# The first attention batch in PSUM slots of three half score tiles with two squares on GpSimd, in place of the fused add-and-relu in h by seven products

## Chip, cores and metric

The kernel runs on one core of a Trainium2 chip. The metric is device time in microseconds (us). Most executions of a kernel agree within 0.3%.

## What is computed

Inputs are q, k and v of shape (8, 12, 448, 64), all fp32, and two weights: moe_w_in (768 x 2048) and moe_w_out (2048 x 768).

```python
scores = (1.0 / np.sqrt(64)) * np.matmul(q, k.transpose(0, 1, 3, 2))
attn = np.maximum(scores, 0.0) ** 2 / 448
x = np.matmul(attn, v)                      # per batch and head
x = x.transpose(0, 2, 1, 3).reshape(8 * 448, 12 * 64)
h = x @ w_in
r = np.maximum(h, 0.0)
out = (r * r) @ w_out                       # (3584, 768) fp32
```

## The kernel before

The kernel works in fp16 with fp32 accumulation. The twelve heads of a batch are three units of four heads, so there are 24 units; a unit has 7 row groups (J = 7). One score tile `t` is one row group of one unit: 128 partitions x two halves (`hh`) x 448 columns. For each, TensorE computes the scores in a PSUM slot (L255), ScalarE evicts them with relu into an fp16 tile `at` (L259), VectorE squares that tile in place (L372), and TensorE multiplies it with v ("AV round", L273 for batch 0, L320 for the others). The AV result is scaled into `xt`, the transposed x of the batch. A score is built of 64 x 64 matmuls, four of which use different quarters of TensorE.

**Batch 0.** q and k of units 0 to 5 are loaded in fp16 by GpSimd's DMA queue (`load16`, L91 to L96; the DMA converts from fp32) and turned by TensorE transposes (`pe_transpose`, L207), which are copied out of PSUM by VectorE (L217). The loop at L792 makes eleven visits of two score tiles. Each `visit` (L374) issues the scores of its tiles twice (`score(t, 2)`, L390), turns units 1 and 2 in between, then runs up to three AV rounds of tiles at least two visits old (`av_some`, L290), and squares the new tiles. Score slots have two PSUM banks, and there are three of them: two of the pool `sps`, one of `third`. The two AV accumulators have one bank each. Between visits 0, 2 and 5 the loop issues the next loads on GpSimd: q and k of units 3, 4 and 5, v of units 3, 4 and 5, and the four parts of w_in (`load_w1`, two DMAs each, L133).

**From batch 0 to the steady part.** After the loop, unit 3 is turned (L807), and weights and later units are loaded. The last AV rounds are interleaved with the first products of h (L827 to L836); then `visit([NB0, NB0 + 1])` issues the first scores of batch 1.

**h and the output.** h of batches 0 and 1 is a plain product (`h_group`, L415). From batch 2 on, h uses seven products instead of eight (`h_period`, L472) over sums of the blocks of w_in and x. There are two periods per batch and so 12 in all, each with 14 steps of six matmuls (L552). A step ends by evicting or adding an accumulator. `plus` (L492) adds a PSUM accumulator and a kept fp32 tile into `g`; it uses a special VectorE operation (L495) that clamps the sum between 0 and 3.4e38, so that relu is part of the addition. `rest` (L499) queues the square of two finished rows of g (L501). Then `o_groups` (L610) multiplies g with w_out (L739), also by seven products, for pairs of batches.

**What sets the order.** The whole program order is written out by hand (`manual_schedule`, L59): each engine, and each DMA queue, runs its instructions in the order in which the code issues them. From L841 on, a planner merges TensorE's steps with events at given times. VectorE's squares are kept in two queues with due times and costs: `due` for the attention squares and `due_g` for those of g. `fill` (L358) puts them where the planned VectorE time has room, `due` first; `flush` and `flush_g` put what must be done.

Of the kernel before, what the change touches and what calls it, by code (L numbers as in the profile page):

```python
# [10 lines left out]

FP16 = mybir.dt.float16
# [6 lines left out]
def kernel(  # L19
# [47 lines left out]
    g_p = ctx.enter_context(tc.tile_pool(name="gp", bufs=1))  # L67
    early = ExitStack()
    q16_p = early.enter_context(tc.tile_pool(name="q16p", bufs=3))

    PSUM = bass.MemoryType.PSUM
    s_p = ctx.enter_context(tc.tile_pool(name="sps", bufs=2, space=PSUM))
    first = ExitStack()
    third_p = first.enter_context(tc.tile_pool(name="third", bufs=1, space=PSUM))
    rounds = ExitStack()
    av_ps = [rounds.enter_context(
        tc.tile_pool(name=f"av{i}ps", bufs=1, space=PSUM, side="right"))
# [3 lines left out]
    def heads(t, n):  # L81
        b, u = divmod(n, NU)
        return t[b].rearrange(
            "(hh u hp) (p j) d -> u (hp p) hh (j d)", hh=2, hp=2, j=J)[u]
# [3 lines left out]
    blks: dict = {}  # L88
    qkt: dict = {}

    def load16(n):  # L91
        tq = q16_p.tile([P, 2, J * D], FP16, name="q16", tag="q16")
        tk = q16_p.tile([P, 2, J * D], FP16, name="k16", tag="k16")
        nc.gpsimd.dma_start(out=tq, in_=heads(q, n))
        nc.gpsimd.dma_start(out=tk, in_=heads(k, n))
        q16s[n] = (tq, tk)  # L96

    def load_v(n):
        t = v_p.tile([P, 2, J * D], FP16, name="vt", tag="vt")
# [51 lines left out]
        dst, x, y = ((t1, b12, b11), (t3, b22, b12), (t2, b22, t1), (nt4, b21, t2))[op]  # L151
        nc.vector.tensor_sub(dst[:, c], x[:, c], y[:, c])

    load16(0)
    ident = const_p.tile([P, P], FP16, name="ident", tag="ident")
    make_identity(nc, ident)
    zeros = const_p.tile([P, S], FP16, name="zeros", tag="zeros")
    nc.vector.memset(zeros, 0.0)
    junk = const_p.tile([P, 1], FP16, name="junk", tag="junk")
    nc.scalar.activation(out=junk, in_=zeros[:, 0:1], func=AF.Relu)  # L160
    load16(1)
    load_v(0)
    load16(2)
    load_v(1)
    load_v(2)

# [23 lines left out]

    big: list = []
    wsum: dict = {}
    slot_no = [0]

    def slot(dtype):
        slot_no[0] += 1
        third = not big and slot_no[0] % 3 == 2 and slot_no[0] < 29
        return (third_p if third else s_p).tile(
            [P, 2, 2048 // mybir.dt.size(dtype)], dtype, name="slot", tag="slot")

    def warm(n):
        ps = slot(FP32)
        for _ in range(n):
            nc.tensor.matmul(ps[:, 0, 0:S], lhsT=zeros[:, 0:P], rhs=zeros,  # L204
                             start=True, stop=True)

    def pe_transpose(n):  # L207
        srcs = q16s.pop(n)
        ts = new_qkt()
        ps = None if n > 3 else slot(FP16)  # L210

        def copy(i, act=False):
            dst, ps = ts[i].rearrange("p j c -> p (j c)"), pss[i][:, i if n < 4 else 0, 0:J * P]
            if act:
                nc.scalar.activation(out=dst, in_=ps, func=AF.Copy)
            else:
                nc.vector.tensor_copy(dst, ps)  # L217

        if n > 3:
            pss = [mm_tile(None, FP16).rearrange("p (i c) -> p i c", i=1) for _ in range(2)]  # L220
        else:
            pss = [ps, slot(FP16) if n == 0 else ps]
        for i, src in enumerate(srcs):
            for j in range(J):
                for hh in range(2):
                    nc.tensor.transpose(  # L226
                        pss[i][64 * hh:64 * hh + 64, i if n < 4 else 0, j * P:(j + 1) * P],
                        src[:, hh, j * D:(j + 1) * D], ident)
            if n == 0:
                copy(i)  # L230
                warm(1)
        qkt[n] = ts
        if n == 3:
            return lambda: (copy(0, True), copy(1))
        if n > 0:
            copy(0, n > 3)
            copy(1)


    xts: dict = {}  # L240
    ats: dict = {}
    seen: dict = {}
    now = [0]
    av_order: deque = deque(range(NU * J))
    avt = [None]

    def score(t, times=1):
        n, j = divmod(t, J)
        qT, kT = qkt[n]
        ps = slot(FP32)  # L250
        for hh in list(range(2)) * times:
            r = slice(64 * hh, 64 * hh + 64)
            for hp in range(2):
                c = slice(64 * hp, 64 * hp + 64)
                nc.tensor.matmul(  # L255
                    ps[c, hh, 0:S], lhsT=kT[r, j, c], rhs=qT[r, :, c],
                    start=True, stop=True)
        at = at_p.tile([P, 2, S], FP16, name="at", tag="at")
        nc.scalar.activation(out=at, in_=ps[:, :, 0:S], func=AF.Relu, scale=SK)  # L259
        ats[t] = at  # L260
        seen[t] = now[0]

    def av_round(t):
        n, j = divmod(t, J)
        b, u = divmod(n, NU)
        vt, at = vts[n], ats.pop(t)
        if j == 0:
            avt[0] = [p.tile([P, 512], FP32, name="avt", tag="av") for p in av_ps]
        ap = avt[0]
        for hp in range(2):  # L270
            r = slice(64 * hp, 64 * hp + 64)
            for hh in range(2):
                nc.tensor.matmul(  # L273
                    ap[hp][64 * hh:64 * hh + 64, 0:S],
                    lhsT=vt[r, hh, j * D:(j + 1) * D], rhs=at[r, hh, :],
                    start=(j == 0), stop=(j == J - 1))
        if j == J - 1:
            if u == 0:
                xts[b] = x_p.tile([P, NM, S], FP16, name="xt", tag="xt")
            for hp in range(2):  # L280
                dst = xts[b][:, 2 * u + hp, :]
                if b < 2 and u == NU - 1 and hp == 0:
                    nc.scalar.activation(
                        out=dst, in_=ap[hp][:, 0:S], func=AF.Copy, scale=CX)
                else:
                    nc.vector.tensor_scalar(  # L286
                        out=dst, in0=ap[hp][:, 0:S],
                        scalar1=CX, scalar2=None, op0=ALU.mult)

    def av_some(lag=2, most=3):  # L290
        done = 0
        while av_order and done < most:
            t = av_order[0]
            if t not in seen or seen[t] > now[0] - lag:
                break
            av_order.popleft()
            av_round(t)
            done += 1
            if t % J == J - 1:
                break  # L300

    unit = [NU]

# [66 lines left out]
    def square(at, lag=0.0):  # L370
        due.append((at_pe[0] + lag, 0.54,
                    lambda: nc.vector.tensor_mul(at, at, at), 0))  # L372

    def visit(tiles, turn=None, lag=2, most=3):  # L374
        now[0] += 1
        for t in tiles:
            if t % J == 0 and t >= NPE * J:
                prefetch(t // J + 2)
        if big:
            for t in tiles[:1]:  # L380
                score(t)
            av_unit()
            for t in tiles[1:]:
                score(t)
            at_pe[0] += 0.19 + 0.19 * len(tiles)
            for i, t in enumerate(tiles):
                square(ats[t], 0.6 + 0.85 * i)
            return
        for t in tiles:
            score(t, 2)  # L390
        if turn is not None:
            pe_transpose(turn)
        flush()
        av_some(lag, most)
        for t in tiles:
            square(ats[t])
        flush()


    gts: dict = {}  # L400
# [71 lines left out]
    def h_period(b, i0, extra):  # L472
# [17 lines left out]
            keep[s, nm] = t.rearrange("p (r c) -> p r c", r=2)  # L490

        def plus(s, y, nm, hi, right):  # L492

            now_ve(0.54)
            nc.vector._custom_dve(  # L495
                TENSOR_ADD_SAT, out=gs(s, hi, right), in0=acc(s, y),
                in1=keep[s, nm], s0=3.4e38, s1=0.0)

        def rest(g, lag):  # L499
            due_g.append((at_pe[0] + lag, 0.54,  # L500
                          lambda: nc.vector.tensor_mul(g, g, g), b))  # L501

        def relu21(s):
            nc.scalar.activation(out=gs(s, True, False), in_=acc(s, 0), func=AF.Relu)  # L504
            rest(gs(s, True), 0.8)

        def c12(s):
            plus(s, 1, "u2", False, True)
            rest(gs(s, False), 0.0)

        def left(k, f, m):

# [274 lines left out]


    NB0 = NU * J
    warm(10)  # L790
    pe_transpose(0)
    for i in range(11):  # L792
        visit([t for t in (2 * i, 2 * i + 1) if t < NB0], turn={1: 1, 4: 2}.get(i))
        if i == 0:
            load16(3)
            load_w1(0)
            load_w1(1)
            load_v(3)
        if i == 2:
            load16(4)  # L800
            load_w1(2)
            load_v(4)
        if i == 5:
            load16(5)
            load_w1(3)
            load_v(5)
    later = pe_transpose(3)  # L807
    load_v(6)
    load_w2(b11, 0, 0)
    load_w2(b12, 0, 1)  # L810
# [4 lines left out]
    first.close()  # L815
    big.append(ctx.enter_context(tc.tile_pool(
        name="mma", bufs=2, space=PSUM, reuse_waits="tile")))

# [2 lines left out]
    def some(part):  # L823
        for _, fn, _ in part:
            fn()

    av_some(1, 9)  # L827
    some(f0[0:2])
    later()
    av_some(0, 9)  # L830
    rounds.close()
    big.append(ctx.enter_context(tc.tile_pool(
        name="mmb", bufs=2, space=PSUM, side="right", reuse_waits="tile")))
    some(f0[2:4])
    some(f1[0:2])
    visit([NB0, NB0 + 1])  # L836

    T_G = NM * 0.1892
# [123 lines left out]
```

## Time and profile before

| | us |
|---|---|
| median of 3 runs (372.5 to 372.99) | 372.75 |
| the profiled execution's own time | 372.5 |
| its span in the profile | 370.7 |
| busy: TensorE matmul | 361.1 |
| busy: VectorE | 266.0 |
| busy: ScalarE | 247.7 |
| busy: GpSimd | 107.1 |
| L259 score evictions, 168 | 145.9, 0.919 each |
| L372 attention squares, 168 | 99.3, 0.618 each |
| L495 additions with relu, 72 | 0.62 each |
| L501 squares of g, 48 | 28.8, 0.618 each |
| L286 xt copies of batch 0, 5 on VectorE | 0.615 each |

Times in the views are microseconds from the start of the span. A line of a timeline gives start, length, engine, line of the kernel, operation, output and inputs with shapes, and the count of instructions merged into it; the bracket at its end is the idle time before it and what ended that. A line of a table by stretches gives the stretch, its length, the engine's busy time in it with the count of instructions, TensorE's granted clock as a share of the full one, the load of the DMA engines and GB/s. PE is TensorE's matmul, PEld its weight load, DVE is VectorE, ACT is ScalarE, POOL is GpSimd.

### The profile page before, as it was taken

Reading aid. Unit: us, or ns where it says so; the run is one execution under the profiler, and the core shown is the slowest. Engines: PE = TensorE matmul, PEld = TensorE weight load, DVE = VectorE, ACT = ScalarE, POOL = GpSimd, SP = SyncE. Lnnn points to the kernel's source line nnn. Section 1 sums busy time; section 2 is a strip of 40 time slices with the busy share of each in tenths; the row PEclk is TensorE's granted clock in tenths of the full one; section 3 lists DMA queues with packets and bytes.
Section 4 is the critical chain, followed back from the end, with each engine's and each line's share of the span. In section 5 each row is a group of like instructions: output and inputs, shape, how many; then the busy total and the mean of one; then the engine's idle time right before and its main releaser. Section 6 shows DMA issues by size and latency. Waiting matters only on the chain.

```text
span 370.7 us, 8742 instructions
## 1 busy us (share of the span) xinstructions
PE 361.1 (97%) x3600; PEld 230.9 (62%) x3600; DVE 266.0 (72%) x470; ACT 247.7 (67%) x370; POOL 107.1 (29%) x128
## 2 busy tenths in 40 slices
PE   8999999999999999999999999999999999999994
PEld 3554444445555778875555588887555689986663
DVE  1886677996767878798575766989756686884442
ACT  2997895786667999876555588887665885532220
POOL 8545531747542355522054045050000000000001
PEclk9999999999999999999999999999999999999998
DMA  8999999999999999969799999592233300002333
GB/s 116 195 204 205 205 204 170 126 146 161 190 170 137 185 106 104 108 90 73 137 136 108 176 162 94 82 104 48 54 82 88 87 1 2 2 0 79 91 91 83
DMA packets 121158, 42.63 MB, mean 115 GB/s; under 512 B 100832, under 2 KB 117760, under 8 KB 121120
## 3 DMA queue, kind: packets, MB, share of 16 engines
q0 software_dynamic: 82912, 23.01, 63.7%
q1 hardware_dynamic: 38048, 18.98, 25.8%
q8 instruction: 28, 0.46, 0.5%
q10 hardware_dynamic: 160, 0.10, 0.1%
q14 instruction: 10, 0.08, 0.1%
HBM read 45.61 MB, written 11.01 MB: 153 GB/s over the span
## 4 chain that ended last, share of the span: by engine, by line
PE 90%; ACT 4%; DVE 3%; issue 1%; POOL 0%; POOLq 0%; ACTq 0%
PE mm L739 34%; PE mm L552 27%; PE slot L255 10%; PE mm L423 9%; PE slot L320 7%; ACT at L259 4%; DVE at L372 1%; PE slot L204 1%; PE slot L226 1%; DVE xt L286 1%; PE mm L226 0%; DVE kT L217 0%; ACT u L641 0%; DVE osb L646 0%; PE avt L273 0%
## 5 line engine op out<-in xcount | busy, mean ns | idle before, releaser
L259 ACT ACTIVATE at<-slot 128x896 f16<-128x896 f32 x168 | 145.9, 919 | 27.9 <-PE slot L255 27.8
L372 DVE TENSOR_TENSOR at<-at 128x896 f16<-128x896 f16 x168 | 99.3, 618 | 12.1 <-ACT at L259 12.0
L109 POOL DMA_DIRECT2D qs<-in_q_dram x36 | 35.3, 983 | 116.5 <-DMA qT<-qs 108.7
L739 PEld LDWEIGHTS <-s 128*128 128x128 f16 x440 | 41.5, 98 | 32.7 <-issue 3.6
L255 PE MATMUL slot<-qT,kT 64*64 64x448 f16 x756 | 57.4, 360 | 1.6 <-ACT at L259 0.9
L552 PEld LDWEIGHTS <-w 128*128 128x128 f16 x576 | 54.3, 98 | 5.1 <-issue 4.3
L552 PE MATMUL mm<-xt,w 128*128 128x224 f16 x432 | 48.9, 259 | 0.0
L739 PEld LDWEIGHTS <-g 128*128 128x128 f16 x336 | 31.7, 98 | 24.1 <-issue 4.7
L552 PEld LDWEIGHTS <-ws 128*128 128x128 f16 x432 | 40.3, 98 | 4.7 <-issue 4.7
L646 DVE SCALAR_TENSOR_TENSOR osb<-mm,u 128x384 f32<-128x384 f32 (+1 forms) x30 | 16.2, 543 | 36.2 <-ACT u L641 23.7
L739 PE MATMUL mm<-b,g 128*128 128x384 f16 x224 | 40.7, 326 | 0.0
L739 PE MATMUL mm<-b,s 128*128 128x384 f16 x216 | 39.6, 326 | 0.2 <-DVE s L608 0.2
L423 PE MATMUL mm<-xt,w 128*128 128x448 f16 x192 | 39.8, 354 | 0.0
L739 PE MATMUL mm<-t,s 128*128 128x384 f16 x224 | 39.3, 326 | 0.0
L255 PEld LDWEIGHTS <-kT 64*64 64x64 f16 x756 | 19.6, 104 | 28.9 <-issue 23.6
L109 POOL DMA_DIRECT2D ks<-in_k_dram x36 | 35.1, 977 | 8.4 <-DMA b<-in_moe_w_out_dram 5.8
L575 POOL DMA_DIRECT2D out_dram<-osb x2 | 1.1, 564 | 119.7 <-DVE osb L646 119.7
L641 ACT ACTIVATE u<-mm 128x384 f32<-128x384 f32 x28 | 13.8, 492 | 31.3 <-PE mm L739 26.8
L552 PE MATMUL mm<-x,ws 128*128 128x224 f16 x288 | 34.1, 259 | 0.0
L495 DVE CUSTOM_DVE_ANT_0 g<-mm,m 128x448 f16<-128x448 f32 x36 | 22.4, 622 | 14.9 <-PE mm L552 7.2
L320 PE MATMUL slot<-at,vt 64*64 64x448 f16 x588 | 31.9, 350 | 0.2 <-DVE at L372 0.2
L501 DVE TENSOR_TENSOR g<-g 128x896 f16<-128x896 f16 x48 | 28.8, 618 | 0.4 <-ACT g L504 0.4
(68 smaller groups left out, 378.1 us busy)
## 6 DMA issues: line engine op xcount, KB each, us to landing
out_dram<-osb SPq DMA_DIRECT2D x52, 192.0 KB, 3.0
vt<-in_v_dram POOLq DMA_DIRECT2D x24, 224.0 KB, 6.0
qs<-in_q_dram POOLq DMA_DIRECT2D x36, 112.0 KB, 4.4
ks<-in_k_dram POOLq DMA_DIRECT2D x36, 112.0 KB, 5.2
w<-in_moe_w_in_dram POOLq DMA_DIRECT2D x8, 384.0 KB, 11.7
b<-in_moe_w_out_dram POOLq DMA_DIRECT2D x4, 768.0 KB, 17.1
q<-in_q_dram POOLq DMA_DIRECT2D x6, 224.0 KB, 7.6
k<-in_k_dram POOLq DMA_DIRECT2D x6, 224.0 KB, 8.1
```

The lines of the kernel that those rows point to most:

```text
L109: nc.gpsimd.dma_start(out=t[:, :, hh, :], in_=heads(src, n)[:, hh].rearrange("p (j d) -> p j d", d=D))
L255: nc.tensor.matmul(ps[c, hh, 0:S], lhsT=kT[r, j, c], rhs=qT[r, :, c], start=True, stop=True)
L259: nc.scalar.activation(out=at, in_=ps[:, :, 0:S], func=AF.Relu, scale=SK)
L320: nc.tensor.matmul(ps[64 * hh:64 * hh + 64, hp, 0:S], lhsT=vt[r, hh, j * D:(j + 1) * D], rhs=at[r, hh, :], start=(j == 0), stop=(j == J - 1))
L372: lambda: nc.vector.tensor_mul(at, at, at), 0))
L423: nc.tensor.matmul(cell[0][:, 0:S], lhsT=w1[f // 4][:, m, (f % 4) * P:(f % 4 + 1) * P], rhs=xts[b][:, m, :], start=(m == 0), stop=(m == NM ...
L495: nc.vector._custom_dve(TENSOR_ADD_SAT, out=gs(s, hi, right), in0=acc(s, y), in1=keep[s, nm], s0=3.4e38, s1=0.0)
L501: lambda: nc.vector.tensor_mul(g, g, g), b))
L552: nc.tensor.matmul(XY[s][y][:, r * Q:(r + 1) * Q], lhsT=left(k, i0 + 2 * s + r, m), rhs=right(k, m), start=(fresh and r == 0 and m == 0), ...
L641: nc.scalar.activation(out=t, in_=X[0][:, 0:HALF], func=AF.Copy, scale=CO)
L646: nc.vector.scalar_tensor_tensor(out=osb[row][:, c], in0=acc[0][:, 0:cc.stop - cc.start], scalar=CO, in1=keep[nm][:, cc], op0=ALU.mult, op ...
L739: nc.tensor.matmul(acc[0][:, 0:HALF], lhsT=left()[:, f], rhs=right[:, f], start=(fresh and f == 0), stop=(f == KH - 1), skip_group_check=n ...
```

## The change

There are two parts. **In h by seven products**, `plus` becomes an ordinary tensor addition, and `rest` queues a relu in SBUF (`tensor_scalar` with max) ahead of each square. After `relu21` it covers only the half that ScalarE has not already put through relu (448 elements per partition), after `c12` both halves (896).

**Batch 0** gets an order of its own in place of the loop of visits. The scores of a unit are 14 halves, packed into slots of three halves (three PSUM banks; two such slots), with one slot of two halves per unit: 15 slots in all. Each slot is evicted by one ScalarE instruction and squared by one instruction, on GpSimd for slots 1 and 3. Unit 0 begins with the seven first halves, so q and k of unit 0 are loaded in two DMAs each, and its first halves are turned and copied apart from its second halves. The transposes of units 0 to 2 use the banks of the AV accumulators. Slots 0 to 4 and slot 14 issue their scores once, the others twice. The AV rounds, `xt` copies and squares stand at written-out places; the first xt half of units 1 and 2 is copied by ScalarE. The pool `sps` is opened only after the first batch's slots are given back. Of the first h products, four instead of two stand ahead of unit 3's transposes, and the last two AV rounds of unit 2 come behind h's first six matmuls.

```diff
     def plus(s, y, nm, hi, right):
-
             now_ve(0.54)
-            nc.vector._custom_dve(
-                TENSOR_ADD_SAT, out=gs(s, hi, right), in0=acc(s, y),
-                in1=keep[s, nm], s0=3.4e38, s1=0.0)
-
-        def rest(g, lag):
-            due_g.append((at_pe[0] + lag, 0.54,
-                          lambda: nc.vector.tensor_mul(g, g, g), b))
+            nc.vector.tensor_add(gs(s, hi, right), acc(s, y), keep[s, nm])
+
+        def rest(g, relu, lag):
+
+            t = at_pe[0] + lag
+            due_g.append((t, 0.32 if relu is g else 0.2, lambda: nc.vector.tensor_scalar(
+                out=relu, in0=relu, scalar1=0.0, scalar2=None, op0=ALU.max), b))
+            due_g.append((t, 0.54, lambda: nc.vector.tensor_mul(g, g, g), b))
...
+    for n, sizes in enumerate(((2, 3, 3, 3, 3), (3, 3, 3, 3, 2), (3, 3, 3, 3, 2))):
+        order = ([(n, j, hh) for hh in range(2) for j in range(J)] if n == 0 else
+                 [(n, j, hh) for j in range(J) for hh in range(2)])
...
+    def new_slot():
+        return s3_p.tile([P, 3, 512], FP32, name="s3", tag="s3")
...
+    def score0(i, ps=None, times=1):
+        ps = new_slot() if ps is None else ps
+        w = len(halves[i])
+        at = at0_p.tile([P, w, S], FP16, name="at0", tag=f"at0_{i}")
+        for _ in range(times):
+            for o, (n, j, hh) in enumerate(halves[i]):
+                qT, kT = qkt[n]
+                r = slice(64 * hh, 64 * hh + 64)
+                for hp in range(2):
+                    c = slice(64 * hp, 64 * hp + 64)
+                    nc.tensor.matmul(
+                        ps[c, o, 0:S], lhsT=kT[r, j, c], rhs=qT[r, :, c],
+                        start=True, stop=True)
+        nc.scalar.activation(out=at, in_=ps[:, 0:w, 0:S], func=AF.Relu, scale=SK)
...
+    def square0(*slots):
+        for i in slots:
+            eng = nc.gpsimd if i in ON_POOL else nc.vector
+            eng.tensor_mul(at0[i], at0[i], at0[i])
...
+    def av0(n, j0, j1):
...
+        for j in range(j0, j1):
             for hp in range(2):
...
+                    nc.tensor.matmul(
+                        ap[hp][64 * hh:64 * hh + 64, 0:S],
+                        lhsT=vt[r, hh, j * D:(j + 1) * D],
+                        rhs=at_of[n, j, hh][r, :],
+                        start=(j == 0), stop=(j == J - 1))
...
-    warm(10)
-    pe_transpose(0)
-    for i in range(11):
-        visit([t for t in (2 * i, 2 * i + 1) if t < NB0], turn={1: 1, 4: 2}.get(i))
...
+    ON_POOL = (1, 3)
...
+    warm(ps, 10)
+    turn(0, (0,))
+    turn_copy(0, 0, LO_P)
+    turn_copy(0, 1, LO_P, slice(0, 2), act=True)
+    turn_copy(0, 1, LO_P, slice(2, J))
+    warm(ps, 2)
+    score0(0, ps)
+    score0(1)
+    turn(0, (1,))
+    turn_copy(0, 0, HI_P)
+    turn_copy(0, 1, HI_P)
+    square0(0)
+    score0(2)
+    square0(1)
+    start_all(load16(3))
+    load_w1(0)
+    load_w1(1)
+    load_v(3)
+    score0(3)
+    square0(2)
+    score0(4)
+    turn(1)
...
+    start_all(load16(4))
+    load_w1(2)
+    load_v(4)
+    square0(3)
+    score0(5, times=2)
...
+    score0(8, times=2)
+    av0(0, 0, 4)
+    square0(8)
+    score0(9, times=2)
+    av0(0, 4, 7)
+    x0(0, 0)
+    x0(0, 1)
+    square0(9)
+    score0(10, times=2)
+    av0(1, 0, 3)
...
+    score0(14)
+    square0(13, 14)
     load_v(6)
...
-    av_some(1, 9)
-    some(f0[0:2])
+    av0(2, 0, 3)
+    some(f0[0:4])
+    av0(2, 3, 5)
+    later = pe_transpose(3)
+    some(f1[0:2])
+    av0(2, 5, 7)
+    x0(2, 0, act=True)
+    x0(2, 1)
     later()
-    av_some(0, 9)
...
-    some(f0[2:4])
-    some(f1[0:2])
     visit([NB0, NB0 + 1])
```

## The prediction

> **What bounds the kernel now.** I read the page first, then the start of each engine's timeline, then VectorE by stage.
>
> The page: TensorE is busy for 97% of the span and carries 90% of the chain that ended last; VectorE and ScalarE are at 72% and 67%.
>
> ```profile
> span 370.7 us, 8742 instructions
> PE 361.1 (97%) x3600; PEld 230.9 (62%) x3600; DVE 266.0 (72%) x470; ACT 247.7 (67%) x370; POOL 107.1 (29%) x128
> PE 90%; ACT 4%; DVE 3%; issue 1%; POOL 0%; POOLq 0%; ACTq 0%
> ```
>
> So from the first h products on, a microsecond moves the end only if it makes TensorE wait or work. The first batch is the other case. ScalarE's timeline shows one unbroken row of 21 score evictions from 8.26 to 26.26 us:
>
> ```profile
> 8.26 8.27 ACT L259 ACTIVATE at<-slot 128x896 f16<-128x896 f32 x10 [6.02 <-PE slot L255]
> 16.87 3.35 ACT L259 ACTIVATE at<-slot 128x896 f16<-128x896 f32 x4 [0.34 <-PE slot L255]
> 20.48 5.78 ACT L259 ACTIVATE at<-slot 128x896 f16<-128x896 f32 x7 [0.27 <-PE slot L255]
> ```
>
> That is 0.827 us each with 0.6 us of gaps: ScalarE bounds the first 26 us. TensorE then reaches the first scores of the second batch (from there on it is full) at 28.57:
>
> ```profile
> 27.70 0.93 PE L423 MATMUL mm<-xt,w 128*128 128x448 f16 x4
> 28.57 0.57 PE L255 MATMUL slot<-qT,kT 64*64 64x448 f16 x8
> ```
>
> The third view is GpSimd's timeline, since the change puts arithmetic into that queue:
>
> ```profile
> 9.79 0.70 POOL L135 DMA_DIRECT2D w<-in_moe_w_in_dram  x1
> 11.22 0.67 POOL L135 DMA_DIRECT2D w<-in_moe_w_in_dram  x1 [0.73 <-DMA vt<-in_v_dram]
> 12.46 0.66 POOL L135 DMA_DIRECT2D w<-in_moe_w_in_dram  x1 [0.57 <-DMA q<-in_q_dram]
> 13.58 0.66 POOL L135 DMA_DIRECT2D w<-in_moe_w_in_dram  x1 [0.46 <-DMA k<-in_k_dram]
> ...
> 20.28 0.66 POOL L135 DMA_DIRECT2D w<-in_moe_w_in_dram  x1 [1.05 <-DMA w<-in_moe_w_in_dram]
> 22.52 0.71 POOL L100 DMA_DIRECT2D vt<-in_v_dram  x1 [1.58 <-DMA w<-in_moe_w_in_dram]
> ```
>
> Number the loads in program order. The 13th (second half of the first w) waits for the 5th (v of unit 0), the 14th for the 6th (q), the 15th for the 7th (k), the 20th for the 12th (w), the 21st (v of unit 4, at 22.52) for the 13th (w). Each load is issued only once the load eight before it has landed, and GpSimd stands still meanwhile. The transfers run at 200 to 206 GB/s from 15 us to 50 us, so these waits are paced by bytes, not by anything the change shortens.
>
> Last, VectorE by stretch (its busy time in each): h of batches 2 and 3, the start and the rest of the products after it, the same for 4 and 5, h of 6 and 7:
>
> ```profile
> 120.00:164.00 44.00, 35.75 (x66) 1.00 1.10 119
> 164.00:176.00 12.00, 10.24 (x20) 1.00 0.85 78
> 176.00:208.00 32.00, 20.96 (x38) 1.00 1.03 136
> 208.00:252.00 44.00, 33.55 (x63) 1.00 0.98 119
> 252.00:264.00 12.00, 11.43 (x21) 1.00 0.05 10
> 264.00:293.00 29.00, 18.55 (x34) 1.00 0.31 75
> 293.00:329.00 36.00, 27.80 (x51) 1.00 0.08 21
> ```
>
> It is 76 to 81% busy in h and up to 95% (11.43 of 12 us) just behind it, with 11 us to spare later in each output stage. In none of these h stages does TensorE wait for VectorE.
>
> **What the Trainium skill says.** *GPSIMD Engine Reference*, Performance versus the Vector engine: a two-input tensor operation on GpSimd takes about 2.6 cycles per element, 4497 ns for 2048 fp32. The trace of before has no such operation; an estimate for 1344 elements is 4497 x 1344/2048 = 2.95 us. *VectorE: DVE Perf Modes*, the perf-mode tier table: a single-source operation on 16-bit SBUF data runs at four elements a cycle, 693 ns for 2048; the trace agrees (the undisturbed copy of 128x2048 at L593 took 684 ns). *TensorE: Matmul & The Clock Gate*, Part 1: a TensorE that idles past some 3.4 us falls to half rate for about as long again. The trace agrees on the two rates: the ten warm-ups take 3.92 us (0.39 each), the same 448 columns later 1.24 us for six (0.21).
>
> **The change, part by part.**
>
> *Start of the first batch.* The four half loads let kT follow after seven transposes instead of fourteen. TensorE is busy warming up till 5.08 us in both kernels. Then I take 0.5 us for the transposes of q, 0.4 for k, 0.6 for the last copy (L217: 0.62), 0.5 for scores and waits: the first eviction at about 6.8 instead of 8.26, 1.4 us earlier. The third slot needs the second halves (transposes behind slot 1's scores, then two copies of 0.62), which costs about 0.9 us back.
>
> *Evictions.* 21 of 128x896 become 12 of 128x1344 and 3 of 128x896. One of 448 columns takes 0.544 (L283), one of 896 takes 0.919 (L259), so 448 columns more cost 0.375, and a wide one in a row 0.827 + 0.375 = 1.20 us. 12 x 1.20 + 3 x 0.827 = 16.9 against 21 x 0.827 = 17.4: 0.5 us saved, and one xt copy more on ScalarE (0.54) takes it back. The scores issued once instead of twice, and the two warm-ups, lie under ScalarE: nothing, as long as ScalarE is the bound.
>
> *The two squares on GpSimd.* Each takes 0.62 us off VectorE, which was not the bound: nothing gained. But GpSimd's queue is in program order. Slot 1's square stands behind the eleven first loads (two issues more than before at 0.7 us each: about 9.7 us) and ahead of q of unit 3. It lasts to 12.7; the transfers queued by then last to about 16 us, so they hardly run dry. **Slot 3's square stands behind v of unit 4.** That is now load 23 and waits for load 15, which is the same second half of the first w: the same bytes are ahead of it, so it is again issued at about 22.5. The square then runs from 22.5 + 0.7 = 23.2 to about 26.1. Bounds: 1.2 us of work (one element a cycle at the page's 1.2 GHz) to 4 us, so an end between 24.4 and 27.2; I take the two-input price.
>
> *Who waits for it.* The AV rounds 0 to 3 of unit 0 stand on TensorE between the scores of slots 8 and 9, and need the second halves of rows 1 to 3: slot 3. TensorE comes there at about 17 us and stops until 26.1. Behind it stand the scores of slots 9 to 14, so ScalarE runs dry too, at about 18.
>
> *Restart, at half rate for three microseconds or so.* Eleven matmuls of the AV rounds in three groups of four at 0.37: 27.2. Slot 9's scores, two groups: 28.0; its eviction ends at 29.0. AV rounds 4 to 6 and slot 10's scores: 30.1; evictions of slots 10 to 13 from 30.3, four at 1.20: 35.1; the xt copy 0.54; slot 14 (two halves) 0.83: **36.4 against 26.26**.
>
> *Handover.* Before, the transposes of unit 3 ran beside the last evictions. Now the first h products come first, in a PSUM bank of slot 14 that its eviction must free, and the transposes, two h products and the last AV rounds queue behind. After the last eviction TensorE has 6 h products (1.2), 4 AV rounds (0.8) and 28 transposes (0.9): 2.9 us. The second batch's scores start at 36.4 + 0.1 + 2.9 = 39.4 against 28.57: **10.8 us later**, with the same work behind them. The matmuls are full from there, so this passes through. I take all of it.
>
> *h by seven products.* 72 sums by the special operation (0.62 us) become plain additions. The trace has no plain addition of that kind; the nearest, L646, takes 0.556 for 384 columns and 0.352 for 192, so 64 more are 64 x 0.204/192 = 0.07: 0.62, no change. What is added are 48 relus in SBUF: 24 of 448 and 24 of 896 elements at four per cycle. From squares of 0.617 that start every 0.54, with 896/2 cycles at that page's 0.96 GHz (0.47), an issue costs about 0.07 beside its streaming; with 448/4 and 896/4 cycles the relus take 0.19 and 0.31 us, 12 us in all, 4 us per h stage. VectorE's spare time there is 44 - 35.75 = 8 us and 8 us in the two others: it fits in sum, but part of the squares already runs into the output stage, where 252 to 264 has 0.6 us left. Of batch 5's leftovers the second output group needs all. I take 1.0 us in all; the bounds are 0 (all of it in gaps) and 6 (half of it exposed); below nothing is excluded, since work is only added.
>
> Sum: 372.5 (the profiled execution: span 370.7 and 1.8 around it; 0.25 below the median 372.75, which I leave out) + 10.8 + 1.0 = 384.3, say **384 us**.
>
> **The rivals.** *A: slot 3's square is through before TensorE asks.* Decides if v of unit 4 is issued by about 14 us. Then the evictions run from 6.8 to about 25.1 (16.9, gap 0.9, xt copy 0.5), the second batch starts at 25.1 + 3.0 = 28.1 instead of 28.57, and the time is 372.5 - 0.5 = 372.0 with the relus hidden: no slower. For it: only three further loads stand between the slot's eviction and that issue in time of GpSimd's own work. Against it: the five waits above, each on the load eight before. Chance 0.08. *B: VectorE becomes the bound in h.* The stall as above, and half the 12 us of relus exposed: 372.5 + 10.8 + 6 = 389.3. For it: 11.43 of 12 us busy at 252 to 264. Against it: no wait on VectorE in h before, and 11 us of room behind. It decides from the point where the squares of the odd batch aren't done when the output group needs them. Chance 0.12. The forecast has 0.80.
>
> **How the numbers follow.** Low end of the forecast: square of 1.2 us (-1.7), restart at full rate (-1.2), handover overlapping by 1 us, relus free (-1.0): 379. High end: square of 4 us (+1), loads run dry for 1.5 us behind the first square, relus 3 us more: 389.5. These hold nine tenths of the forecast's 0.80 and over half of B's: 0.79. The measurement tells 0.2% (0.7 us) from no change. Only A ends below 373.5: half of its 0.08 faster, a quarter within 0.2%; slower 0.94.
>
> **What would show it.** GpSimd's square of the fourth slot starting near 23 us, right behind the issue of v of unit 4; TensorE and ScalarE idle from about 18 to 26; the first eviction near 6.8, fifteen in all, the wide ones 1.2 us apart; the second batch's scores near 39; relus of 0.2 to 0.4 us on VectorE and TensorE still without waits in h. If that square starts before 17 us, the forecast is wrong and A holds.

## Result and the profile after

| | us |
|---|---|
| before, median of 4 runs (372.5 to 374.43) | 372.87 |
| changed, median of 4 runs (387.94 to 389.76) | 389.19 |
| ratio, 95% interval | 1.0425 (1.0386 to 1.0464) |
| the changed kernel's profiled execution, and its span | 387.94, 386.2 |

The change makes the kernel 16.3 us slower. The prediction was 384, slower, with a range of 379 to 389.5.

The page of the changed kernel shows where to look: TensorE's busy time grows by 5.4 us while the span grows by 15.5, its third slice of 9.7 us is busy for only three tenths, and 2% of the chain that ended last is now a transfer of w and 4% GpSimd.

```profile
span 386.2 us, 8707 instructions
PE 366.5 (95%) x3568; PEld 233.9 (61%) x3568; DVE 279.6 (72%) x511; ACT 248.5 (64%) x366; POOL 112.0 (29%) x132
...
PE   8838799999999999999999999999999999999995
...
PEclk9678999999999999999999999999999999999999
...
PE 82%; DVE 4%; ACT 4%; POOL 4%; DMA 2%; issue 2%; POOLq 0%; DVEq 0%; ACTq 0%
```

GpSimd's timeline has the two squares (L294), each of about 2.5 us; the second follows the load of v of unit 4, which waited for w:

```profile
9.01 2.51 POOL L294 TENSOR_TENSOR at<-at 128x1344 f16<-128x1344 f16 x1
11.38 0.78 POOL L94 DMA_DIRECT2D q<-in_q_dram  x1
...
21.37 0.66 POOL L135 DMA_DIRECT2D w<-in_moe_w_in_dram  x1 [1.15 <-DMA w<-in_moe_w_in_dram]
23.28 0.71 POOL L100 DMA_DIRECT2D vt<-in_v_dram  x1 [1.25 <-DMA w<-in_moe_w_in_dram]
24.00 2.44 POOL L294 TENSOR_TENSOR at<-at 128x1344 f16<-128x1344 f16 x1
```

TensorE's timeline has the wait that this makes: five AV matmuls at 19.5, then nothing until GpSimd is done. It also has a second one that the prediction lacks, 2.1 us ahead of the second batch's scores:

```profile
19.50 0.54 PE L329 MATMUL avt<-at,vt 64*64 64x448 f16 x5
26.49 1.33 PE L329 MATMUL avt<-at,vt 64*64 64x448 f16 x11 [6.46 <-POOL at L294]
...
40.55 0.57 PE L329 MATMUL avt<-at,vt 64*64 64x448 f16 x8
43.22 0.57 PE L246 MATMUL slot<-qT,kT 64*64 64x448 f16 x8 [2.10 <-DVE kT L213]
```

Those scores started at 28.57 before. The delay there is 14.65 us, and it is passed on unchanged: h of batches 2 and 3 begins 14.65 us later as well (L552 before, L583 after). Two places add to it. Behind h of batches 4 and 5, the fifth group of eight matmuls waits for a sum. These are the same group before and after:

```profile
262.26 1.46 PE L739 MATMUL mm<-b,s 128*128 128x384 f16 x8
277.80 1.47 PE L770 MATMUL mm<-b,s 128*128 128x384 f16 x8 [0.72 <-DVE s L639]
```

TensorE's waits on such sums come to 0.9 us in the steady part, against 0.2 before. The start of the last output stage loses another 0.3 us. Behind the last matmul 0.5 us are regained, so that the span grows by 15.5 us.

### The profile page after: what moved, and what is told of

It is laid out like the page before. It is cut to its first block, busy times and chain, and to the rows that moved or that the text cites. A ratio compares the mean times of both kernels' runs of the same rounds, so it can differ in the third digit from the quotient of the medians.

```text
span 386.2 us, 8707 instructions
## 1 busy us (share of the span) xinstructions
PE 366.5 (95%) x3568; PEld 233.9 (61%) x3568; DVE 279.6 (72%) x511; ACT 248.5 (64%) x366; POOL 112.0 (29%) x132
## 4 chain that ended last, share of the span: by engine, by line
PE 82%; DVE 4%; ACT 4%; POOL 4%; DMA 2%; issue 2%; POOLq 0%; DVEq 0%; ACTq 0%
PE mm L770 30%; PE mm L583 24%; PE mm L453 9%; PE slot L246 9%; PE slot L361 7%; DMA w<-in_moe_w_in_dram 2%; ACT at L250 2%; PE avt L329 1%; ACT at L286 1%; DVE s L639 1%; DVE at L413 1%; POOL k L94 1%; POOL q L94 1%; DVE g L531 1%; POOL at L294 1%
## 5 line engine op out<-in xcount | busy, mean ns | idle before, releaser
L250 ACT ACTIVATE at<-slot 128x896 f16<-128x896 f32 x147 | 128.5, 918 | 21.7 <-PE slot L246 21.7
L413 DVE TENSOR_TENSOR at<-at 128x896 f16<-128x896 f16 x147 | 86.9, 618 | 8.8 <-ACT at L250 8.8
L583 PEld LDWEIGHTS <-w 128*128 128x128 f16 x576 | 54.3, 98 | 5.2 <-issue 4.3
L583 PE MATMUL mm<-xt,w 128*128 128x224 f16 x432 | 49.0, 259 | 0.0
L246 PE MATMUL slot<-qT,kT 64*64 64x448 f16 x588 | 46.1, 362 | 2.6 <-DVE kT L213 2.1
L583 PEld LDWEIGHTS <-ws 128*128 128x128 f16 x432 | 40.3, 98 | 4.7 <-issue 4.7
L583 PE MATMUL mm<-x,ws 128*128 128x224 f16 x288 | 34.1, 259 | 0.0
L531 DVE TENSOR_TENSOR g<-g 128x896 f16<-128x896 f16 x48 | 29.8, 621 | 1.2
L246 PEld LDWEIGHTS <-kT 64*64 64x64 f16 x588 | 14.3, 104 | 26.0 <-issue 20.8
L524 DVE TENSOR_TENSOR g<-mm,m 128x448 f16<-128x448 f32 x36 | 22.2, 621 | 10.5 <-PE mm L583 6.9
```

What stands on the lines that cost most here:

```text
L246: nc.tensor.matmul(ps[c, hh, 0:S], lhsT=kT[r, j, c], rhs=qT[r, :, c], start=True, stop=True)
L524: nc.vector.tensor_add(gs(s, hi, right), acc(s, y), keep[s, nm])
L531: due_g.append((t, 0.54, lambda: nc.vector.tensor_mul(g, g, g), b))
L583: nc.tensor.matmul(XY[s][y][:, r * Q:(r + 1) * Q], lhsT=left(k, i0 + 2 * s + r, m), rhs=right(k, m), start=(fresh and r == 0 and m == 0), ...
```

## The experiments

All medians are of several runs beside runs of the kernel before on the same chip (372.4 to 372.6 us). Each ratio is to those. The changed kernel ran beside a kernel before at 372.87, so a difference between the medians of two experiments can be wrong by some 0.3 to 0.4 us.

**1. Slot 3's square moved ahead of the loads of unit 4.** The same instruction on the same engine, at another place in its queue:

```diff
+    square0(3)
     start_all(load16(4))
     load_w1(2)
     load_v(4)
-    square0(3)
```

> Queue theory: slot 3's square costs time only because it stands behind the load of v of unit 4 in GpSimd's program order, not because GpSimd computes it. Moved ahead of the loads of unit 4, it starts near 16.8 us and ends near 19.3, before TensorE asks at about 20. The wait of 6.5 us is gone, and with it part of the restart at half rate: 389.2 - 6.5 to - 8.0 = 381 to 383 us. Rival (GpSimd is simply too slow for the square, or the loads that are now issued 2.5 us later hold something up): still 387 or more. Rival (the written-out order itself costs the time): 387 or more.

Measured: 380.57 us, ratio to before 1.0215 (1.0202 to 1.0228), so 8.6 us less than the changed kernel. GpSimd's timeline has the square behind v of unit 3:

```profile
17.26 2.49 POOL L294 TENSOR_TENSOR at<-at 128x1344 f16<-128x1344 f16 x1
```

TensorE's timeline of the same run has 0.18 us of the wait left:

```profile
19.80 0.76 PE L329 MATMUL avt<-at,vt 64*64 64x448 f16 x11 [0.18 <-POOL at L294]
```

So half of the loss hangs on the place of this one square in the queue, with GpSimd's speed unchanged (2.49 us). The other half, 8.0 us, remains, and a part of it still comes from GpSimd's squares, as run 2 shows.

**2. All fifteen squares on VectorE.**

```diff
-    ON_POOL = (1, 3)
+    ON_POOL = ()
```

> All fifteen squares on VectorE. Queue theory: the wait is gone as in the run with the earlier square, 381 to 383 us; and as VectorE's square of slot 2 no longer waits for GpSimd's of slot 1 (9.2 to 11.9 us in the changed kernel), unit 1's copies and the fifth slot come up to 1.8 us earlier: 379.5 to 382. Rival (two squares more make VectorE late): not below the run with the earlier square.

Measured: 380.91 us, ratio 1.0225 (1.0212 to 1.0239): in the range, but not below run 1, as its rival had foreseen. The expectation named the wrong slot. In the changed kernel it is VectorE's square of slot 0 that runs beside GpSimd's of slot 1, and it takes four times as long as when GpSimd has no square. The changed kernel's group from 5 to 16 us (count, busy time, mean ns):

```profile
L294 DVE TENSOR_TENSOR at<-at 128x896 f16<-128x896 f16 x1 | 2.8, 2786 | 0.0
```

The same group in this run:

```profile
L294 DVE TENSOR_TENSOR at<-at 128x896 f16<-128x896 f16 x1 | 0.6, 626 | 0.0
```

In the changed kernel's profiled execution that square held nothing up: unit 1's first copy started at 13.03 us, as here (13.02), and waited for its transposes. So the gain of up to 1.8 us that was expected there did not come.

The second GpSimd square does cost time. In run 1 it ran from 17.26 to 19.75 us, and the VectorE square that began at 17.94 took 2.54 us, the three behind it 0.85 each. The xt copies (L340) behind them came late, and TensorE waited 1.1 us for them. VectorE's timeline in run 1:

```profile
17.94 4.85 DVE L294 TENSOR_TENSOR at<-at 128x1344 f16<-128x1344 f16 x4
22.70 1.15 DVE L340 TENSOR_SCALAR xt<-avt 128x448 f16<-128x448 f32 x2
```

The same place in this run:

```profile
17.93 2.58 DVE L294 TENSOR_TENSOR at<-at 128x1344 f16<-128x1344 f16 x3
...
21.61 1.15 DVE L340 TENSOR_SCALAR xt<-avt 128x448 f16<-128x448 f32 x2
```

The xt copies start 1.1 us earlier, and so do the second batch's scores (34.73 against 35.82). In the profiled execution this is lost again: TensorE, after its 2.1 us of idling, runs the next twelve h products at half rate (3.91 us against 2.44 in run 1). That this is also why the medians agree is not shown.

**3. The fused addition back in h.** The changed kernel with `plus` and `rest` of before.

```diff
-            nc.vector.tensor_add(gs(s, hi, right), acc(s, y), keep[s, nm])
+            nc.vector._custom_dve(
+                TENSOR_ADD_SAT, out=gs(s, hi, right), in0=acc(s, y),
+                in1=keep[s, nm], s0=3.4e38, s1=0.0)
...
-            due_g.append((t, 0.32 if relu is g else 0.2, lambda: nc.vector.tensor_scalar(
-                out=relu, in0=relu, scalar1=0.0, scalar2=None, op0=ALU.max), b))
```

> The changed kernel with the clamping addition of before in h and no separate relu. From the two traces the relus cost 0.9 us at the start of the output products of batches 4 and 5 and 0.45 us at those of 6 and 7: 389.2 - 1.3 = 387.9 us. Rival (VectorE is the bound in h): 384 or less. Rival (the relus fit in gaps): within 0.3 of 389.2.

Measured: 387.83 us, ratio 1.0407 (1.0394 to 1.0421): 1.4 us less than the changed kernel (1.1 when each is taken against the kernel before beside it), though the two intervals overlap. TensorE's wait for the sums in the steady part falls from 0.9 to 0.2 us.

**4. Only the relu part, in the kernel before.** The reverse edit, made in the kernel before.

```diff
-            nc.vector._custom_dve(
-                TENSOR_ADD_SAT, out=gs(s, hi, right), in0=acc(s, y),
-                in1=keep[s, nm], s0=3.4e38, s1=0.0)
+            nc.vector.tensor_add(gs(s, hi, right), acc(s, y), keep[s, nm])
```

> The kernel before with only the plain addition and the separate relu in h. If the two parts of the change add up: 372.9 + 1.3 = 374.2 us. Rival (the first batch's delay shifts the work behind it and makes the relus dearer there): 373.2 or less here. Rival (VectorE is the bound in h): 378 or more.

Measured: 374.15 us, ratio 1.0048 (1.0032 to 1.0063): 1.5 us, clear of no change. In its trace the same wait appears, 0.9 us in two instances for the sums. The additions themselves take 0.62 us in both kernels. So the 48 relus cost 1.1 to 1.5 us, wherever the first batch ends, and as far as the overlapping intervals of run 3 tell, the two parts of the change add up.

**5. The dose: the square further back.**

```diff
     load_v(4)
-    square0(3)
...
     load_w1(3)
+    square0(3)
     load_v(5)
```

> The dose: slot 3's square is put further back in GpSimd's queue, behind q and k of unit 5 and the last part of w_in. Those loads are paced by the landing of the load eight before; the last of them is issued near 29.4 to 30 us in the changed kernel. Queue theory: the square runs from about 30.0 to 32.5, TensorE waits to 32.5 instead of 26.5, and the time grows by the same 6.0: 395 us (394 to 396). Rival (something else than the square's place holds TensorE there): within 1 of 389.

Measured: 394.03 us, ratio 1.0581 (1.0567 to 1.0596): 4.8 us more than the changed kernel (5.1 against the kernels before beside them), at the low end of the range. In the profiled execution the square ran from 31.04 to 33.48, so that TensorE went on at 33.53 and not at 26.49:

```profile
33.53 1.33 PE L329 MATMUL avt<-at,vt 64*64 64x448 f16 x11 [13.41 <-POOL at L294]
```

TensorE's restart moved by 7.0 us, and that execution's span by the same 7.0 (393.2 against 386.2). The changed kernel's profiled execution is the fastest of its four and this one the slowest of its four, so the medians differ by less. The direction and the mechanism hold; why the medians differ by less than 6.0 is not settled.

**6. The handover.** Run 1's kernel with unit 3's transposes and their copies ahead of the first h products:

```diff
     av0(2, 0, 3)
+    later = pe_transpose(3)
+    later()
     some(f0[0:4])
     av0(2, 3, 5)
-    later = pe_transpose(3)
     some(f1[0:2])
     av0(2, 5, 7)
     x0(2, 0, act=True)
     x0(2, 1)
-    later()
```

> The run with the earlier square, and in it unit 3's transposes and their two copies put ahead of the first h products instead of behind them. In that run TensorE idled 2.1 us before the second batch's scores, for the copy of kT, which stood behind the xt copies on ScalarE and VectorE. Handover theory: the idle is gone, the scores start near 33.4 instead of 35.8: 380.6 - 2.4 = 378.2 us. Rival (the copies only change places with the xt copies, and TensorE waits for xt instead): 380 or more.

Measured: 378.52 us, ratio 1.0162 (1.0146 to 1.0177): 2.1 us less than run 1. In run 1 TensorE's timeline has the wait:

```profile
35.82 0.57 PE L246 MATMUL slot<-qT,kT 64*64 64x448 f16 x8 [2.10 <-DVE kT L213]
```

In this run it has the scores right behind the AV rounds, without a wait:

```profile
35.32 0.57 PE L329 MATMUL avt<-at,vt 64*64 64x448 f16 x8
35.73 0.55 PE L246 MATMUL slot<-qT,kT 64*64 64x448 f16 x8
```

In this one execution, the slowest of the five (380.58), they start no earlier than in run 1 (35.82), because its first batch's evictions ended 0.9 us later and its transposes of unit 3 ran at half rate (0.96 us for fourteen against 0.58). The medians carry the verdict; the trace shows only that the wait is gone.

**7. All the named costs taken out.** On VectorE all squares, run 6's handover, run 3's addition, and two moves more:

```diff
     score0(3)
+    turn(1)
+    turn_copy(1, 0)
+    turn_copy(1, 1)
     square0(2)
     score0(4)
-    turn(1)
-    turn_copy(1, 0)
-    turn_copy(1, 1)
...
-    av0(1, 0, 3)
     square0(10)
     score0(11, times=2)
-    av0(1, 3, 4)
+    av0(1, 0, 4)
```

> All the costs that the traces name taken out together, the new slots kept: all squares on VectorE, the handover as in the run beside it, unit 1 turned one slot earlier (ScalarE idled 2.3 us for its copies), the AV rounds of unit 1 that wait for the xt copies put behind slot 11's scores (1.2 us), and the fused addition in h. From the run with all squares on VectorE: last eviction at 29.3 - 2.2 - 1.2 = 25.8, the second batch's scores at about 28.9 against 28.6 before: 373 us (372 to 375), no faster than before. Rival (the wide slots are worth their saving once nothing else is in the way): 371.5 or less. Rival (they cost something that isn't named yet): 376 or more.

Measured: 373.43 us, ratio 1.0021 (1.0013 to 1.0028). The 16.3 us are found but for 0.8. ScalarE's timeline has the new slots at work, with gaps of 0.2 to 0.8 us between rows and the last eviction's end at 26.06 (26.26 before):

```profile
9.40 2.47 ACT L287 ACTIVATE at<-s 128x1344 f16<-128x1344 f32 x2 [0.75 <-PE s L284]
12.19 3.65 ACT L287 ACTIVATE at<-s 128x1344 f16<-128x1344 f32 x3 [0.32 <-PE s L284]
16.29 3.28 ACT L287 ACTIVATE at<-s 128x1344 f16<-128x1344 f32 x3 [0.45 <-PE s L284]
19.80 5.01 ACT L287 ACTIVATE at<-s 128x1344 f16<-128x1344 f32 x4 [0.22 <-PE s L284]
24.69 0.55 ACT L339 ACTIVATE xt<-avt 128x448 f16<-128x448 f32 x1
25.12 0.94 ACT L287 ACTIVATE at<-s 128x896 f16<-128x896 f32 x1
```

The second batch's scores start at 29.26 against 28.57:

```profile
29.26 0.55 PE L247 MATMUL slot<-qT,kT 64*64 64x448 f16 x8
```

An eviction that starts at 6.55 instead of 8.26 is used up in the gaps, the extra xt copy and the work left behind the last eviction (3.2 us to the second batch's scores, 2.3 before).

**8 and 11. TensorE kept busy during its wait.** The changed kernel with 22, then 31 matmuls of zeros ahead of the AV rounds that wait.

```diff
         ap = avt[0]
+        for _ in range(22 if n == 0 and j0 == 0 else 0):
+            nc.tensor.matmul(ap[0][:, 0:S], lhsT=zeros[:, 0:P], rhs=zeros,
+                             start=True, stop=True)
```

> The changed kernel with 22 matmuls of zeros ahead of the AV rounds that wait for slot 3, into the accumulator that those rounds then start afresh, so that TensorE is busy for 4.6 us of its wait. Restart theory: part of the 16.3 us is the half rate after the wait; without it slot 10's eviction starts near 29.0 instead of 31.2 and the time falls by 2 to 2.5: 387 us (386 to 388). Rival (the rate after the wait doesn't matter, ScalarE's evictions set the pace): within 0.6 of 389.2.

> As the run with 22 matmuls of zeros, with 31: that run left TensorE idle for 2.8 us after them and its rate fell all the same, so it did not decide. 31 take 6.0 us at full rate and reach to about 26 us. Restart theory: AV rounds and scores behind the wait now run at full rate, slot 10's eviction starts near 29.2 instead of 31.2, 387 us (386 to 387.8). Rival (the rate after the wait doesn't matter): within 0.6 of 389.2.

Measured with 22: 387.9 us, ratio 1.0411 (1.0385 to 1.0436). The number lies in the range, but it decides nothing: TensorE idled 2.8 us behind the zeros, and the rate fell during the restart (granted clock 0.71 from 25 to 30 us). With 31: 387.03 us, ratio 1.0402 (1.0383 to 1.0421). TensorE's granted clock is the number behind GpSimd's count. In the changed kernel the stretches from 25 to 35 us are:

```profile
25.00:30.00 5.00, 3.51 (x40) 2.25 (x41) 0.33 (x1) 0.92 (x1) 4.14 (x5) 0.50 1.26 204
30.00:35.00 5.00, 4.63 (x75) 3.52 (x67) 3.04 (x5) 3.44 (x3) 0.74 (x2) 0.82 1.25 205
```

With 31 matmuls of zeros they are:

```profile
25.00:30.00 5.00, 3.88 (x60) 2.05 (x62) 1.49 (x3) 1.65 (x2) 4.05 (x5) 1.00 1.26 204
30.00:35.00 5.00, 3.69 (x66) 2.23 (x59) 3.13 (x5) 4.29 (x5) 2.03 (x4) 1.00 1.25 205
```

The clock is 1.00 in both stretches against 0.50 and 0.82. The second batch's scores start at 41.63 instead of 43.22, though the wait ended at 26.80 instead of 26.49: from the restart to these scores it is 14.8 us instead of 16.7. So half rate cost 1.9 us there. The medians differ by 2.2 us (1.7 against the kernels before beside them), but the intervals of the two ratios overlap.

**9. The mended kernel (run 7's) with slots 1 and 3 on GpSimd again**, slot 3's ahead of the loads of unit 4:

```diff
-    ON_POOL = ()
+    ON_POOL = (1, 3)
...
+    square0(3)
     start_all(load16(4))
     load_w1(2)
     load_v(4)
-    square0(3)
```

> The mended kernel with its squares of slots 1 and 3 on GpSimd again, slot 3's ahead of the loads of unit 4. Queue theory: it still stands behind v of unit 3, issued at 16.0 to 16.8, so it ends near 19.2, where TensorE now asks for it at 16.5: 2 to 2.5 us later than the mended kernel, 375.7 us (375 to 376.5). Rival (GpSimd relieves VectorE): 373 or less.

Measured: 375.82 us, ratio 1.0097 (1.0083 to 1.011), 2.4 us more than run 7. The square of slot 3 ran from 17.14 to 19.58 behind v of unit 3 (16.41), and TensorE waited for it:

```profile
19.63 0.76 PE L330 MATMUL avt<-at,vt 64*64 64x448 f16 x11 [1.70 <-POOL at L295]
```

VectorE's square of slot 0 took 2.78 us again, and the one beside slot 3's took 3.47. In this batch the two squares on GpSimd cost time even at a better place.

**10. The xt copy on VectorE.** The mended kernel of run 7 with one argument less:

```diff
-    x0(1, 0, act=True)
+    x0(1, 0)
```

> The mended kernel with the first xt half of unit 1 copied by VectorE instead of ScalarE, where it stood behind two evictions while TensorE idled 1.2 us for it. ScalarE has 0.4 us less to do ahead of the last slot, and the transposes follow that eviction: 373.4 - 0.5 = 372.9 us (372.5 to 373.2), level with the kernel before. Rival (VectorE's queue is as late as ScalarE's): 373.4 or more.

Measured: 373.45 us (372.93 to 376.88), ratio 1.0038 (1.0016 to 1.0059). A miss: no gain over run 7, as its rival had foreseen. TensorE's wait of 1.23 us for that copy is gone, but in the profiled execution TensorE fell to half rate at 16 us (0.96 us for fourteen transposes) and ScalarE idled 1.26 us for the scores behind it. Whether the copy's place is worth anything stays open. No version of the wide slots beat the kernel before.

## Why the prediction was right in kind and short in size

**The load eight before** held as predicted. v of unit 4 was issued at 23.28 (predicted 22.5), the square ran from 24.00 to 26.44 (predicted 23.2 to 26.1). Runs 1 and 5 show that the place in the queue is the cause: forward and back, the time follows.

**The square's price.** The estimate from the Trainium skill (*GPSIMD Engine Reference*, Performance versus the Vector engine) was 2.95 us; the trace has 2.48. The measurement decides. The prediction had given no cost to the two squares beside their place. That was incomplete: a square on GpSimd holds up one on VectorE. Beside the square of slot 1, VectorE's of slot 0 took 2.79 us instead of 0.62. In the changed kernel nothing waited for it, but in run 1 such a hold cost 1.1 us. The Trainium skill has a reason in *SBUF — State Buffer*, Who interferes with whom: a VectorE operation with two SBUF inputs and a GpSimd operation that reads SBUF share a port pair that only one of them has at a time, and the other stops. The traces agree: the held square ended 0.50 us behind GpSimd's in the changed kernel, where 0.62 us is its usual time, and in runs 1 and 9 (a wider one, usually 0.85) 0.73 and 0.72 us behind it.

**TensorE's arrival.** Predicted at 17 us, measured 20.0. The sixth slot's eviction (slot 5, the first of unit 1) began late, while unit 1 was transposed, at half rate, and copied:

```profile
16.20 2.47 ACT L286 ACTIVATE at<-s 128x1344 f16<-128x1344 f32 x2 [2.77 <-PE s L283]
```

The prediction had ScalarE running without a gap from the third slot on. The late arrival made the wait shorter (6.5 us and not 9). It did not move the end of the wait, which GpSimd sets.

**The restart.** Predicted from 26.1 to the last eviction's end at 36.4, 10.3 us; measured from 26.49 to 37.76, 11.3. The half rate was foreseen, but for three microseconds; the granted clock was 0.50 till about 31.8 us (an estimate from its mean of 0.82 in 30 to 35 us), 5.3 us behind the restart, and run 11 puts its cost at 1.9 us where the prediction's low end had 1.2. The condition that the prediction took from *TensorE: Matmul & The Clock Gate*, Part 1, idling past some 3.4 us, is not met in every case here: in run 8 half rate followed an idle time of 2.8 us, and from 12 to 18 us the changed kernel's clock was 0.50 with no idle time above 0.82 us before it. The measurement decides.

**The handover is the term that was mis-sized most.** The prediction said 2.9 us of matmuls and 0.1; it measured 43.22 - 37.76 = 5.5, of which 2.1 are TensorE's wait and 3.4 its work. Counted were TensorE's instructions, not the copies that the second batch's scores need: qT on ScalarE and kT on VectorE stand behind the last xt copies, which wait for the last AV rounds, and kT starts when qT is through. ScalarE's timeline:

```profile
41.15 0.54 ACT L338 ACTIVATE xt<-avt 128x448 f16<-128x448 f32 x1 [3.40 <-PE avt L329]
41.59 0.91 ACT L211 ACTIVATE qT<-slot 128x896 f16<-128x896 f16 x1
```

VectorE's timeline:

```profile
41.20 0.62 DVE L340 TENSOR_SCALAR xt<-avt 128x448 f16<-128x448 f32 x1 [2.78 <-PE avt L329]
42.54 0.63 DVE L213 COPY kT<-slot 128x896 f16<-128x896 f16 x1 [0.71 <-ACT qT L211]
```

Run 6 takes the wait out, for 2.1 us. The delay of 10.8 us became 14.65 through three terms: 0.4 for the later end of the square, 1.0 for the restart and 2.5 for the handover.

**The relus.** Predicted 1.0 us at the start of the output stages; runs 3 and 4 give 1.1 to 1.5. They took 0.386 and 0.272 us each; as with the squares, 0.08 of that lies beside the next instruction, which leaves the predicted 0.31 and 0.19. TensorE waited for a sum in the stage that was named. VectorE's stretch behind h of batches 4 and 5, moved by 15 us, has 0.4 us left where it had 0.6:

```profile
267.00:279.00 12.00, 11.61 (x25) 1.00 0.09 18
```

**The range** held by 0.3 us, and that was luck in part. Its high end was made of a square of 4 us, loads that run dry and dearer relus, and none of these came. What came, the copies in the handover and the longer half rate, stood in no high end. The rest of the distance from 384.3 is spread: the profiled execution took 387.94, and the median is 1.25 us above it.

**Rival A** (no wait at slot 3, level with before) had the right question and a wrong price. Run 1 is that case but for 0.18 us, and it takes 380.6, not 372.0. Its working took the wide slots to run without gaps and the handover at 3 us. **Rival B** (VectorE bounds h) did not occur: run 3 gives back 1.4 us, not 6.

In sum: over the kernel before on its own chip, the changed kernel loses 16.3 us, run 1 8.0, run 6 5.9 and run 7 0.8. So 8.4 us go to the square's place with the restart behind it, 2.0 to the handover, 5.1 to the rest of run 7's edits, and 0.8 are left over. Of the 5.1 some 1.4 are the relus; squares on VectorE, unit 1's turn and the AV rounds of unit 1 share the other 3.7 and are not told apart.

## What to carry to other kernels

Arithmetic put into a queue that also issues loads inherited the pace of the loads here: before placing such work, find which transfer the issue ahead of it waits for, and when that lands, and compare that with the time at which the result is asked for. Count a handover by what its first instruction reads, not by the matmuls ahead of it. And price a rival as carefully as the forecast: what was "otherwise as planned" held half of the loss here.

## What was not expected of the hardware

A square of 128x896 on VectorE took 2.79 us instead of 0.62 while GpSimd squared another tile, and the time shows as a longer instruction, not as idle time. A copy out of PSUM is not held in this way: in run 1 VectorE's copy of kT at 17.41 us ran beside GpSimd's square and took 0.61.

TensorE's rate fell to half during a stretch in which it idled only 0.8 us at a time. The changed kernel from 10 to 15 us:

```profile
10.00:15.00 5.00, 3.46 (x46) 2.09 (x45) 4.63 (x5) 3.42 (x3) 4.89 (x7) 0.63 1.24 192
```

Run 1, with the same instructions up to there:

```profile
10.00:15.00 5.00, 2.62 (x46) 1.56 (x46) 4.94 (x6) 3.65 (x3) 4.93 (x5) 1.00 1.21 184
```

In run 1 TensorE idled more, up to 1.35 us at a time, and kept the full rate. From 12 to 18 us the clock was also 0.50 in runs 3 and 5, and 1.00 in runs 8 and 11, all with the same instructions up to the wait. So this differs between executions; what decides it, and what it costs by itself, is not shown.
